# Gradients of shift and scale of the second LayerNorm from column sums in the MLP phase, and gW1 from modulated rows

## The chip, the core and the metric

The kernel runs on one core of a Trainium2 chip. The metric is the device time of one execution in microseconds; several executions are timed and the median is given. A profile of one more execution shows what each engine did. The engines are PE (matrix multiplies; weight loads are listed apart as PEld), DVE (vector), ACT (scalar functions), POOL, and SP, which in this kernel issues every DMA transfer, one after the other in one queue.

## The reference

One block with two branches, forward and backward. `x` is 2048 x 512, the hidden size of the MLP is 1792; everything is bfloat16, the sums fp32.

```python
sa, ca, ga, sb, cb, gb = split(silu(c) @ w_mod)            # six rows of 512
x1  = x  + ga * A(layernorm(x)  * (1 + ca) + sa)           # A: irfft2(rfft2(h) * W)
n2  = layernorm(x1)
h2  = n2 * (1 + cb) + sb                                   # modulated rows
hid = relu(h2 @ w1 + b1) ** 2
out = x1 + gb * (hid @ w2 + b2)
# outputs: out, and the gradients of x, w_r, w_i, w1, b1, w2, b2, c, w_mod for a given grad_out
```

With `gh` for the gradient at the input of the ReLU (2048 x 1792) and `G = gh @ w1.T` for that of `h2`, the gradients of `w1`, of the shift `sb` and of the scale `cb` are

```python
gW1 = h2.T @ gh
gsb = column sums of G            # = sum over f of w1[d, f] * gb1[f],  gb1 = column sums of gh
gcb = column sums of G * n2       # = sum over f of w1[d, f] * (n2.T @ gh)[d, f]
```

The equalities in the comments are the two ways in which the kernels get them.

## The kernel before

The rows are cut into 16 tiles t of 128 rows, and these into 4 blocks b of 4 tiles (SB = 512 rows). The hidden size is 14 tiles fc of 128. A tile scheduler takes the program as it is written in Python, gives each instruction its priority from there and puts each engine's instructions in an order by its own model; the engines then run these lists in order, and SP's list is the order of the transfers. `merge` interleaves lists of pieces, `Delayed(n)` holds n pieces back until later ones come.

In time the kernel has these parts: the forward spectral branch and the product of grad_out with w2 (to about 95 us), the MLP phase (95 to 321), the backward spectral branch with the gradient of w1 between its steps (321 to 424, here the gW1 phase), and the rest: the last inverse transform, the gradient of w2 and that of w_mod (424 to 514).

*MLP phase.* First w1T (the transposed w1, 14 x 128 x 512) is prepared on DVE: times (1 + cb), less its mean over the row (L685 to L691), so that a product with it comes out as the gradient of the normalized row less its mean. Then, per block:

- `stage_h` (L762): 56 matmuls of 128x128 by 512 (L770) into the two PSUM accumulators `mm`, ReLU on ACT (L771), square and product on DVE (L773, L777), both written to DRAM (L778, L779). Its operand h2T is the block's modulated rows, transposed.
- `stage_o` (L829): row tiles of the MLP's output (L788, L790), evicted by ACT (`o`, L842), multiplied by grad_out to `gp` and added to x1, which goes out at L853. Between its pieces runs `stage_g` (L707) of the next block: the last two steps of the forward transform (psT, psY, helper lines L332 to L346), y on ACT (L717), then x1, mean, variance and the normalized rows n2rows on DVE (L734), written to DRAM at L736.
- `stage_gn` (L792): 56 matmuls with w1T (L790, form `og<-w1T,gab`), scaled on ACT to cb (L806), then DVE: a dot product with n2rows (L809), gx1 (L811, L815), the product qy (L820). Between them `stage_t` (L740) of the next block transposes n2rows on PE, 16 tiles into `pst` (L746); DVE (L749) and ACT (L751) evict them with scale and shift: that is h2T.
- `colsums` (L679): three rows (gp, qy, grad_out) summed over the tile into three quadrants of one PSUM tile `acc`.

In the last blocks the first step of the backward transform (`spec_f1_row`) is interleaved as well; for the first two blocks `f1_again` (L858) loads gx1 back from DRAM (L865).

*gW1 phase.* 16 units `grad_w1(fb, dc)` (L941), each 16 matmuls of 128x128 by 448 (L948) with the rows n2 (`n2_sb`, 2 MB, loaded at L986) as operand. DVE makes from the accumulator gW1 (L954, with `gtmp` from ACT L952) and its product with a slice of w1 (`w1s`, loaded per unit), summed to gcb (L956); a third product (L960) gives gsb. `grad_b1` (L921) sums gh over the rows ahead of each four units. The spectral steps of a group gi are psB (L274), AE on ACT (L281, L283), psC (L261) with the factors LFb (L977), G on ACT (L263), and complex products on DVE with the loaded Z and Xb. Two units follow each group from the second on (`fill_w1`), and two are left for the end phase.

*End phase.* A loop over t with the last transform; `fill` puts one piece of `grad_w2` (L1022) into each step, and every second time one row's share of w_mod's gradient (`gm.emit`, L406 to L425). `grad_mod_mid` (L1032) turns the sums gsb and gcb, which lie in columns, into rows first.

Of the kernel before, what the change touches and what calls it, by code (L numbers as in the profile page):

```python
# [428 lines left out]
def kernel(  # L429
# [9 lines left out]
    n2_dram = dram.tile([P, NT, D], BF16, name="n2_dram")  # L439
# [28 lines left out]
    modb = constp.tile([P, 4, D], BF16, name="modb")  # L468
    GA_B, GB_B, CA1_B, CB1_B = range(4)
# [70 lines left out]
    srow = p0.tile([1, 2, D], BF16, name="srow")  # L540

    def mod_row(j):
# [3 lines left out]
        if j in (1, 4):  # L546
            nc.vector.tensor_scalar(modb[:, CA1_B if j == 1 else CB1_B, :], ps, 1.0, None, op0=ALU.add)
        elif j in (2, 5):
            nc.scalar.copy(out=modb[:, GA_B if j == 2 else GB_B, :], in_=ps)
        else:  # L550
            nc.scalar.copy(out=srow[:, j // 3, :], in_=ps[0:1, :])
# [36 lines left out]
    for i in range(4):  # L588
        nc.tensor.matmul(psc[:, i, :], lhsT=srow[:, 0, i * P:(i + 1) * P],
                         rhs=pm, start=True, stop=True)  # L590
# [9 lines left out]
    for i, row in enumerate((srow[:, 1, :], modb[0:1, CB1_B, :], modb[0:1, GB_B, :])):  # L600
# [66 lines left out]
    b2row = wp.tile([1, D], BF16, name="b2row")  # L667
    nc.sync.dma_start(b2row, B_b2[None, :])
    rows = tc.alloc_tile_pool(name="rows", bufs=2)
    hring = tc.alloc_tile_pool(name="hring", bufs=8)  # L670
# [3 lines left out]
    with tc.tile_pool(name="psR", bufs=1, space=PSUM) as psR, tc.tile_pool(name="psO", bufs=2, space=PSUM) as psO_pool, \  # L674
# [4 lines left out]
        def colsums(t, *trio):  # L679
            for i, row in enumerate(trio):  # L680
# [3 lines left out]

        nmean = wp.tile([P, NFC], FP32, name="nmean")  # L685
        for fc in range(NFC):
            nc.vector.scalar_tensor_tensor(out=w1T[:, fc, :], in0=w1T[:, fc, :], scalar=K["onef"], in1=modb[:, CB1_B, :], op0=ALU.mult, op1=ALU.mult,
                                           accum_out=nmean[:, fc:fc + 1])
        nc.vector.tensor_scalar(nmean, nmean, -1.0 / D, None, op0=ALU.mult)
        for fc in range(NFC):  # L690
            nc.vector.tensor_scalar(w1T[:, fc, :], w1T[:, fc, :], nmean[:, fc:fc + 1], None, op0=ALU.add)  # L691

        h2T, n2b, x1b, yb, hT, gbt, qys, gps = ({} for _ in range(8))
        ghn = [None] * NB
        late = Delayed(2)
# [11 lines left out]
        def stage_g(b):  # L707
# [13 lines left out]
            def norm(j):  # L721
# [10 lines left out]
                rstd_act(nc, inv2[:, t:t + 2], mv[:, :, 1], K)  # L732
                for i in range(2):
                    nc.vector.tensor_scalar(n2b[b][:, j + i, :], x1[:, i, :], mv[:, i, 0:1], inv2[:, t + i:t + i + 1], op0=ALU.subtract, op1=ALU.mult)  # L734
# [3 lines left out]
            return [lambda f=f, j=j: f(j) for j in range(TB) for f in (g2, g3)]  # L738
# [23 lines left out]
        def stage_h(b):  # L762
            sl = slice(b * SB, (b + 1) * SB)
            load_rows(b + 1)
            for fc in range(0, NFC, 2):
# [13 lines left out]
                nc.sync.dma_start(gh_dram[fc * P:(fc + 2) * P, sl].rearrange("(a p) s -> p a s", p=P), gh)  # L779

        def sums(t):
            if t in gps and t in qys:
                for t in (t, t + 1):
                    late.add(lambda t=t: colsums(t, gps[t], qys[t], gbt[t // TB][:, t % TB, :]))
# [7 lines left out]
        def stage_gn(b, ub=None):  # L792
            P_, st = {}, {}

            def half(j, h):
                t = TB * b + j
                if j % 2 == 0 and h == 0:
                    st["gx1"] = rows.tile([P, 2, D], BF16, name="gx1")
                    st["cb"] = rows.tile([P, 2, D], BF16, name="cb", bufs=3)
# [3 lines left out]
                if h == 0:  # L803
                    return
                i, gx1, cb, n2row, gb = j % 2, st["gx1"], st["cb"], n2b[b][:, j, :], gbt[b]
                nc.scalar.activation(cb[:, i, :], P_.pop(j), AF.Copy, scale=inv2[:, t:t + 1])  # L806
                jk = rows.tile([P, D], BF16, name="jk", bufs=1)
                rb = rows.tile([P, 1], FP32, name="rb")
# [358 lines left out]
```

## Time and profile before

| | before |
|---|---|
| median of 3 runs | 516.03 us (514.89 to 520.2) |
| profiled execution, its own time | 516.24 us |
| its span, first to last instruction | 514.5 us |
| mean granted clock of PE | 0.954 |
| busy: PE / DVE / ACT | 453.1 / 363.1 / 239.5 us |
| bytes moved by DMA | 99.39 MB |

The profile gives names of tiles as the program has them, without buffer numbers; where a name ends in a digit the digit is left out too (n2_sb shows as n_sb, w1s as w1s). A wait of an engine is put down to the instruction that ended it. The granted clock is the share of full speed at which PE was let run in a window.

### The profile page before, as it was taken

The numbers are of one execution on the slowest core, as the hardware profiler recorded it, in microseconds if no ns is written. First come the engines' busy times: TensorE is split into PE (matmuls) and PEld (weight loads), VectorE is DVE, ScalarE is ACT, GpSimd is POOL, SyncE is SP. The second block draws the span as 40 slices with busy tenths as digits, with TensorE's granted clock in tenths as the row PEclk, the third lists the DMA queues.
The fourth block names the chain that finished last, engine by engine and source line by source line (L and its number), as shares of the span: only waits on it lengthen the run. The fifth ranks groups of instructions, "written<-read, shape, count | busy, mean of one in ns | idle before, by whom it ended". The sixth has DMA issues, their size and how long they took to land.

```text
span 514.5 us, 7304 instructions
## 1 busy us (share of the span) xinstructions
PE 453.1 (88%) x2507; PEld 226.1 (44%) x2507; DVE 363.1 (71%) x862; ACT 239.5 (47%) x415; POOL 12.5 (2%) x56
## 2 busy tenths in 40 slices
PE   0868999999999999989999799766986999879995
PEld 0434466554434444444444344543442465434342
DVE  5877899685479863867487462357796578469986
ACT  3455766683551361455237232653222257627424
POOL 4111100000000000000000000000000000000000
PEclk9957999999999999999999889889998899989998
DMA  8954859921394495399039746676556519988997
GB/s 286 235 159 97 328 139 295 336 73 42 119 302 151 134 295 145 125 199 331 22 111 249 233 109 137 193 237 150 142 139 219 169 45 280 236 256 263 250 261 234
DMA packets 148062, 99.39 MB, mean 193 GB/s; under 512 B 93363, under 2 KB 134841, under 8 KB 147385
## 3 DMA queue, kind: packets, MB, share of 16 engines
q1 hardware_dynamic: 148024, 98.93, 68.8%
q8 instruction: 19, 0.31, 0.2%
q14 instruction: 19, 0.15, 0.1%
HBM read 37.26 MB, written 39.61 MB: 149 GB/s over the span
## 4 chain that ended last, share of the span: by engine, by line
PE 56%; DVE 17%; DMA 11%; SPq 8%; ACT 5%; issue 3%; DVEq 0%; ACTq 0%
PE og L790 16%; PE mm L770 9%; PE mm L621 7%; PE mm L948 6%; PE psG L301 3%; SPq L516 3%; DMA w1s<-in_B_w_dram 2%; PE psY L346 2%; PE psT L332 2%; PE psB L274 2%; SPq L518 2%; PE psC L261 2%; DVE jk L1092 2%; DMA n<-n_dram 1%; DVE gm_junk L423 1%
## 5 line engine op out<-in xcount | busy, mean ns | idle before, releaser
L948 PE MATMUL mm<-gab,n_sb 128*128 128x448 bf16 x256 | 54.4, 372 | 5.7 <-DVE gjk L956 5.7
L621 PE MATMUL mm<-gT,w2T 128*128 128x512 bf16 x224 | 55.4, 380 | 1.9 <-DVE gab L624 1.6
L790 PE MATMUL og<-w1T,gab 128*128 128x512 bf16 x224 | 54.2, 391 | 0.0
L770 PE MATMUL mm<-h2T,w 128*128 128x512 bf16 x224 | 52.8, 378 | 0.1
L1025 PE MATMUL mm<-g_sb,hn 128*128 128x512 bf16 x224 | 51.9, 381 | 0.0
L790 PE MATMUL og<-w,h 128*128 128x512 bf16 x224 | 51.4, 380 | 0.0
L771 ACT ACTIVATE r<-mm,b1col 128x512 bf16<-128x512 f32 x56 | 38.2, 688 | 13.1 <-PE mm L770 9.4
L948 PEld LDWEIGHTS <-n_sb 128*128 128x128 bf16 x256 | 26.0, 102 | 33.9 <-issue 14.0
L770 PEld LDWEIGHTS <-w 128*128 128x128 bf16 x224 | 21.3, 97 | 28.4 <-issue 6.7
L790 PEld LDWEIGHTS <-gab 128*128 128x128 bf16 x224 | 22.1, 101 | 24.8 <-issue 3.6
L621 PEld LDWEIGHTS <-w2T 128*128 128x128 bf16 x224 | 21.5, 98 | 25.3 <-issue 5.9
L1025 PEld LDWEIGHTS <-hn 128*128 128x128 bf16 x224 | 21.1, 98 | 26.1 <-issue 3.8
L790 PEld LDWEIGHTS <-h 128*128 128x128 bf16 x224 | 20.8, 98 | 26.0 <-issue 2.9
L624 DVE CAST gab<-mm 128x512 bf16<-128x512 f32 x28 | 19.2, 687 | 15.6 <-PE mm L621 15.4
L773 DVE TENSOR_TENSOR h<-r 128x1024 bf16<-128x1024 bf16 x28 | 19.3, 690 | 15.0 <-ACT r L771 14.9
L842 ACT CAST o<-og 128x512 bf16<-128x512 f32 x16 | 9.4, 586 | 42.6 <-PE og L790 42.6
L847 DVE TENSOR_TENSOR gp<-gb,o 128x1024 bf16<-128x1024 bf16 x8 | 5.5, 689 | 28.7 <-ACT o L842 28.7
L335 ACT ACTIVATE Tsb<-psT 128x512 bf16<-128x512 f32 x32 | 18.3, 600 | 14.2 <-PE psT L332 14.1
L954 DVE SCALAR_TENSOR_TENSOR gw<-mm,mcol,gtmp 128x448 bf16<-128x448 f32 x16 | 10.9, 681 | 19.5 <-PE mm L948 18.5
L626 ACT CAST gab<-mm 128x512 bf16<-128x512 f32 x28 | 16.4, 586 | 16.2 <-PE mm L621 16.2
L806 ACT ACTIVATE cb<-og,inv 128x512 bf16<-128x512 f32 x16 | 11.0, 688 | 26.8 <-PE og L790 26.8
L952 ACT ACTIVATE gtmp<-gb1bc,mcol 128x448 f32<-128x448 bf16 x16 | 10.3, 665 | 22.8 <-DVE gw L954 22.7
(270 smaller groups left out, 813.7 us busy)
## 6 DMA issues: line engine op xcount, KB each, us to landing
h_dram<-h SPq DMA_DIRECT2D x28, 256.0 KB, 3.1
gh_dram<-gab SPq DMA_DIRECT2D x28, 256.0 KB, 3.3
w<-in_B_w_dram SPq DMA_DIRECT2D x2, 1792.0 KB, 8.0
wm<-in_w_mod_dram SPq DMA_DIRECT2D x3, 1024.0 KB, 8.9
wmc<-in_w_mod_dram SPq DMA_DIRECT2D x12, 256.0 KB, 4.4
out_dram<-gwm SPq DMA_DIRECT2D x12, 256.0 KB, 3.9
xs_dram<-Xs SPq DMA_DIRECT2D x8, 258.0 KB, 3.0
Xb<-xs_dram SPq DMA_DIRECT2D x8, 258.0 KB, 3.0
```

Source lines behind the costliest of these rows:

```text
L301: nc.tensor.matmul(ps[:, ch, :], lhsT=Z[gi][:, hh, ri, ch:256:2], rhs=K["LG"][:, n, ri:ri + 2, :].rearrange("p y m -> p (y m)"), start=(ri ...
L335: nc.scalar.activation(Tsb, ps, AF.Copy, scale=EF_S)
L516: nc.sync.dma_start(gT[b][:, :, j * P:(j + 1) * P], g_view[:, TB * b + j, :], transpose=True)
L621: nc.tensor.matmul(ps, lhsT=w2T[:, dc, fc * P:(fc + 1) * P], rhs=gT[b][:, dc, :], start=(dc == 0), stop=(dc == 3))
L624: nc.vector.tensor_copy(out=gaT[b][:, fc, :], in_=ps)
L626: nc.scalar.copy(out=gaT[b][:, fc, :], in_=ps)
L770: nc.tensor.matmul(ps, lhsT=w1[:, dc, (fc + i) * P:(fc + i + 1) * P], rhs=h2T[b][:, dc, :], start=(dc == 0), stop=(dc == 3))
L771: nc.scalar.activation(r[:, i, :], ps, AF.Relu, bias=b1col[:, fc + i:fc + i + 1])
L773: nc.vector.tensor_tensor(h2, r, r, op=ALU.mult)
L790: nc.tensor.matmul(ps, lhsT=lhs(fc), rhs=rhs[:, fc, :], start=(fc == 0 and init is None), stop=(fc == NFC - 1))
L948: nc.tensor.matmul(ps[:, 0:W4], lhsT=n2_sb[:, t, dc * P:(dc + 1) * P], rhs=ghn[t // 4][:, t % 4, fs], start=(t == 0), stop=(t == NT - 1))
L1025: nc.tensor.matmul(ps, lhsT=hns[fc][:, t, :], rhs=g_sb[:, t, :], start=(t == 0), stop=(t == NT - 1))
```

## The change

1. *MLP phase.* w1T stays as loaded. `stage_gn` evicts the plain product G (the gradient of the modulated row) on ACT; a new function `norm_back` works on two tiles at a time and makes q2 = G * n2 and v = G * (1 + cb), takes the mean of v (ACT, with an accumulator) and the dot product with n2 (DVE), and puts gx1 together from n2, scaled and shifted by ACT, from v and from grad_out. `colsums` takes four rows (gp, qy, G, q2), so that sums 3 and 4 are gsb and gcb.
2. `stage_g` makes n2 on ACT, and on DVE two products more, the modulated rows h2r, which are written to DRAM (h2_dram) in pairs. For blocks 1 to 3 h2T is read from there by a transposing DMA, one for each tile; block 0 stays with `stage_t`. The transposing loads of gh (`ghn_part`) move from `stage_o` to `stage_gn`. The first products of `late` are held in two lists, both emptied after the third pair of `stage_h`; `f1_again` loads two pairs ahead. The buffers of h go from 8 to 7, those of gp from 3 to 2.
3. *gW1 phase.* The units use the modulated rows (`h2_sb`), so their accumulator is gW1 itself: one ACT copy, and one write for two units. The slices w1s and the three DVE passes go. Each four units' `grad_b1` comes after them, not ahead.
4. *End phase.* The sums of shift and scale are rows already. Grad_out's column sums (for b2's gradient), no longer summed in the MLP phase, become 16 matmuls of their own (`grad_b2`). Five rows of w_mod's gradient are in the list (gms) instead of four entries, so one more stands behind the loop.

The core of the diff:

```diff
-        def colsums(t, *trio):
-            for i, row in enumerate(trio):
+        def colsums(t, *quad):
+            for i, row in enumerate(quad):
...
-        for fc in range(NFC):
-            nc.vector.scalar_tensor_tensor(out=w1T[:, fc, :], in0=w1T[:, fc, :], scalar=K["onef"], in1=modb[:, CB1_B, :], op0=ALU.mult, op1=ALU.mult,
-                                           accum_out=nmean[:, fc:fc + 1])
...
                 for i in range(2):
-                    nc.vector.tensor_scalar(n2b[b][:, j + i, :], x1[:, i, :], mv[:, i, 0:1], inv2[:, t + i:t + i + 1], op0=ALU.subtract, op1=ALU.mult)
-                if j == TB - 2:
-                    nc.sync.dma_start(n2_dram[:, TB * b:TB * b + TB, :], n2b[b])
+                    nc.scalar.activation(n2b[b][:, j + i, :], x1[:, i, :], AF.Identity, bias=nb[:, i:i + 1], scale=inv2[:, t + i:t + i + 1])
...
+                nc.vector.tensor_tensor(h2r, n2b[b][:, j:j + 2, :], modb[:, CB1_B, None, :].broadcast_to([P, 2, D]), op=ALU.mult)
+                nc.vector.tensor_tensor(h2r, h2r, modb[:, SB_B, None, :].broadcast_to([P, 2, D]), op=ALU.add)
+                nc.sync.dma_start(h2_dram[:, t:t + 2, :], h2r)
+                if b > 0:
+                    for i in range(j, j + 2):
+                        nc.sync.dma_start(h2T[b][:, :, i * P:(i + 1) * P], h2_dram[:, TB * b + i, :], transpose=True)
...
+                if h == 1:
+                    nc.scalar.copy(out=st["G"][:, j % 2, :], in_=P_.pop(j))
+                    if j % 2 == 1:
+                        norm_back(t - 1, j - 1)
+
+            def norm_back(t, j):
...
+                nc.vector.tensor_tensor(q2, G, n2, op=ALU.mult)
+                nc.vector.tensor_tensor(v, G, cb1[:, None, :].broadcast_to([P, 2, D]), op=ALU.mult)
+                for i in range(2):
+                    nc.scalar.activation(v[:, i, :], v[:, i, :], AF.Copy, scale=i2[:, i:i + 1], accum_out=rr[:, 0, i:i + 1])
+                    nc.vector.scalar_tensor_tensor(out=jk[:, i, :], in0=q2[:, i, :], scalar=K["onef"], in1=cb1, op0=ALU.mult, op1=ALU.mult,
+                                                   accum_out=rr[:, 1, i:i + 1])
...
+                for i in range(2):
+                    nc.scalar.activation(n2[:, i, :], n2[:, i, :], AF.Identity, scale=rr[:, 1, i:i + 1], bias=rr[:, 0, i:i + 1])
+                nc.vector.tensor_tensor(v, v, gb, op=ALU.add)
+                gx1 = n2
+                nc.vector.tensor_tensor(gx1, gx1, v, op=ALU.add)
...
-            nc.vector.scalar_tensor_tensor(out=gw, in0=ps[:, 0:W4], scalar=mcol[:, CB1_C, dc:dc + 1], in1=tmp, op0=ALU.mult, op1=ALU.add)
...
-            nc.vector.scalar_tensor_tensor(out=jk, in0=ps[:, 0:W4], scalar=K["onef"], in1=w1s, op0=ALU.mult,
-                                           op1=ALU.mult, accum_out=gcba[:, dc, fb:fb + 1])
...
+        nc.scalar.copy(out=w1o[0][:, fb % 2, :], in_=ps[:, 0:W4])
+        if fb % 2 == 1:
+            nc.sync.dma_start(out4_view[:, dc, (fb - 1) * W4:(fb + 1) * W4], w1o[0].rearrange("p a f -> p (a f)"))
...
-        nc.sync.dma_start(n2_sb, n2_dram)
+        nc.sync.dma_start(h2_sb, h2_dram)
...
+    def grad_b2():
+        ps = psX.tile([P, D], FP32, name="mm")
+        for t in range(NT):
+            q = 32 * (t % 4)
+            nc.tensor.matmul(ps[q:q + 32, :], lhsT=K["ones_q"], rhs=g_sb[:, t, :], start=(t < 4), stop=(t >= 12), tile_position=(0, q))
+        add_quadrants(ps, gwp, out_7[None, :], modb[0:1, GB_B, :])
```

The scheduler's lists move with it. At the change from block 2 to block 3, ACT's list (L806 is the eviction of the w1 product, L807 in the new kernel; L771 and L772 are the ReLU of stage_h; utcs belongs to the first spectral step). Before:

```order
L806 ACTIVATE cb<-og,inv_70 128x512
L751 ACTIVATE h2T<-pst_2860,mcol 128x512
L806 ACTIVATE cb<-og,inv_70 128x512
L239 CAST utcs<-psY 128x64x8
L751 ACTIVATE h2T<-pst_2893,mcol 128x512
L806 ACTIVATE cb<-og,inv_70 128x512
L771 ACTIVATE r<-mm,b1col 128x512 x4
L239 CAST utcs<-psT 128x64x8
L239 CAST utcs<-psY 128x64x8
L771 ACTIVATE r<-mm,b1col 128x512 x10
```

and after (v and n2rows are written by norm_back):

```order
L807 CAST G<-og 128x512 x2
L822 ACTIVATE v,rr<-v,inv_70 128x512 x2
L807 CAST G<-og 128x512
L828 ACTIVATE n2rows<-n2rows,rr 128x512 x2
L807 CAST G<-og 128x512
L239 CAST utcs<-psY 128x64x8
L822 ACTIVATE v,rr<-v,inv_70 128x512 x2
L772 ACTIVATE r<-mm,b1col 128x512 x2
L828 ACTIVATE n2rows<-n2rows,rr 128x512 x2
L772 ACTIVATE r<-mm,b1col 128x512 x4
```

Four passes of norm_back stand among the first ReLUs. On PE, in the new kernel, the first column sum (gp) stands ahead of the 56 matmuls of stage_h, and those of y, G and q2 of the first pair behind the second of them, at each of the block changes (at the third with a piece of the spectral step on v ahead of them).

SP's list ahead of the same change, where the rows of block 3 are written (L736; in the new kernel h_dram<-h2r stands for h2_dram, L734, and the transposes into h2T are L737; out_dram<-x is stage_o's output, gx_dram the gradient of the rows, gab<-gh_dram the transposing loads of gh). Before:

```order
L853 DMA out_dram<-x_2043 128x1024 x2
L736 DMA n_dram<-n2rows 128x2048
L816 DMA gx_dram<-gx_2778 128x1024
L865 DMA gx_3082<-gx_dram 128x1024
L760 DMA_TRANSPOSE gab<-gh_dram 128x4x256 x4
```

and after:

```order
L869 DMA out_dram<-x_2025 128x1024
L880 DMA o<-gx_dram 128x1024
L734 DMA h_dram<-h2r 128x1024
L737 DMA_TRANSPOSE h2T<-h_dram 128x4x128 x2
L869 DMA out_dram<-x_2025 128x1024
L880 DMA o<-gx_dram 128x1024
L734 DMA h_dram<-h2r 128x1024
L737 DMA_TRANSPOSE h2T<-h_dram 128x4x128 x2
L832 DMA gx_dram<-n2rows 128x1024
L761 DMA_TRANSPOSE gab<-gh_dram 128x4x256 x6
```

What h2T needs goes through this queue now, each half behind a write of stage_o's output.

SP's list at the start of the gW1 phase (n_sb is n2_sb, h_sb is h2_sb; LFb, Z and Xb are operands of the spectral steps). Before:

```order
L977 DMA LFb<-LF_dram 128x768 x2
L493 DMA Z_3387<-in_A_w_r_dram 64x2x257
L493 DMA Z_3387<-in_A_w_r_dram 32x2x257 x2
L493 DMA Z_3387<-in_A_w_i_dram 64x2x257
L493 DMA Z_3387<-in_A_w_i_dram 32x2x257 x2
L980 DMA Xb<-xs_dram 128x1032
L493 DMA Z_3388<-in_A_w_r_dram 64x2x257 x2
L493 DMA Z_3388<-in_A_w_i_dram 64x2x257 x2
L980 DMA Xb<-xs_dram 128x1032
L986 DMA n_sb<-n_dram 128x8192
```

and after:

```order
L869 DMA out_dram<-x_2460 128x1024
L989 DMA LFb<-LF_dram 128x768 x2
L998 DMA h_sb<-h_dram 128x8192
L869 DMA out_dram<-x_2460 128x1024
L989 DMA LFb<-LF_dram 128x768 x3
L493 DMA Z_3384<-in_A_w_r_dram 64x2x257
L493 DMA Z_3384<-in_A_w_r_dram 32x2x257 x2
L493 DMA Z_3384<-in_A_w_i_dram 64x2x257
L493 DMA Z_3384<-in_A_w_i_dram 32x2x257 x2
L992 DMA Xb<-xs_dram 128x1032
```

The 2 MB of rows for gW1 now come ahead of Z and Xb and of all but two pieces of LFb.

More of the change, by code (lines that the diff above doesn't have):

```diff
@@ L963 @@
     units = []
-    for fb in range(NFB):
+    for fp in range(0, NFB, 2):
         for dc in range(4):
-            units.append(lambda fb=fb, dc=dc: (dc == 0 and grad_b1(fb), grad_w1(fb, dc)))
+            for fb in (fp, fp + 1):
+                units.append(lambda fb=fb, dc=dc: (grad_w1(fb, dc), dc == 3 and grad_b1(fb)))
     def fill_w1(n):
@@ L1030, in grad_w2 @@
         load_hn()
-    def grad_mod_mid(i, j):
-        psr = psX.tile([P, D], FP32, name="mm")
-        for dc in range(4):
-            nc.tensor.matmul(psr[0:1, dc * P:(dc + 1) * P], lhsT=colsb[:, i, dc:dc + 1], rhs=K["ident"], start=True, stop=True)
-        row = gwp.tile([1, D], BF16, name="gmrow")
-        nc.scalar.copy(out=row, in_=psr[0:1, :])
-        gm.emit(j, 0, row, endp["gm"], psX)
+    def grad_b2():
[4 more added lines that the diff above has]
+        add_quadrants(ps, gwp, out_7[None, :], modb[0:1, GB_B, :])
     load_hn()
```

163 lines of the change are left out of this document (77 added, 86 removed).

## The prediction

> **What bounds the kernel now.** I read the page first, then the windows of three long stretches, then the waits of PE in the one where PE is least busy, and last the timeline around its longest gaps.
>
> ```profile
> span 514.5 us, 7304 instructions
> PE 453.1 (88%) x2507; PEld 226.1 (44%) x2507; DVE 363.1 (71%) x862; ACT 239.5 (47%) x415; POOL 12.5 (2%) x56
> 321.00:424.00 103.00, 83.38 (x542) 46.51 (x540) 69.81 (x157) 38.63 (x67) 0.00 (x0) 0.92 0.56 161
> ```
>
> In the last line stand the window, its length, then busy time of PE, its weight loads, DVE, ACT and POOL, the granted clock of PE, the DMA share and GB/s. PE is the bound as a whole, so what counts is where PE stands idle or runs at a lower clock. The gW1 phase (321 to 424) is the weak place: 83.38 of 103 us busy, at a granted clock of 0.92. The waits of PE in it, and four rows of its timeline (start, duration, in brackets the idle time before):
>
> ```profile
> PE psB L274 <- ACT AE L283: 6.1, 5, 2.2
> PE mm L948 <- DVE gjk L956: 5.7, 2, 4.0
> PE psC L261 <- ACT G L263: 2.3, 1, 2.3
> PE mm L934 <- DVE gjk L956: 1.8, 2, 1.3
> PE psC L261 <- DMA LFb<-LF_dram: 1.6, 1, 1.6
> PE mm L935 <- DVE b4l L932: 1.4, 2, 1.3
> PE mm L927 <- DVE gjk L956: 0.7, 1, 0.7
> 346.25 6.22 PE L948 MATMUL mm<-gab,n_sb 128*128 128x448 bf16 x32
> 357.95 7.90 PE L948 MATMUL mm<-gab,n_sb 128*128 128x448 bf16 x32 [1.66 <-DVE gjk L956]
> 397.28 7.96 PE L948 MATMUL mm<-gab,n_sb 128*128 128x448 bf16 x28 [4.04 <-DVE gjk L956]
> 396.53 0.69 DVE L956 SCALAR_TENSOR_TENSOR gjk<-mm,onef,w1s 128x448 bf16<-128x448 f32 x1 [3.52 <-DMA w1s<-in_B_w_dram]
> ```
>
> The seven waits are 19.6 us. Those on DVE are 5.7 + 1.8 + 1.4 + 0.7 = 9.6: a PSUM accumulator of gW1 comes free only after the product L956, and that product waits for the slice w1s (the last row: 3.52 us, behind which the 4.04 us gap of PE stands). Those on the spectral chain (ACT, and the LFb load) are 10.0. Behind a gap the same work is also slower: 32 matmuls take 6.22 us, but 7.90 after the gap of 1.66 (1.68 lost), and 28 take 7.96 after 4.04, where 28/32 of 6.22 is 5.44 (2.5 lost). So 4.2 us of clock loss belong to the DVE gaps, 13.8 us together.
>
> **gW1 phase.**
>
> ```profile
> 366.45 0.75 PE L927 MATMUL mm<-gab,ones_q 128*32 128x448 bf16 x12
> n_sb<-n_dram SPq DMA_DIRECT2D x1, 2048.0 KB, 8.8
> L842 ACT CAST o<-og 128x512 bf16<-128x512 f32 x16 | 9.4, 586 | 42.6 <-PE og L790 42.6
> ```
>
> The three DVE passes over each unit (L954, L956, L960), gtmp on ACT and the w1s loads go; an ACT copy of PSUM comes. The 13.8 us go with their cause. The copy of 448 columns is at most the 0.59 us that one of 512 takes (L842): 14 units in the phase give ACT some 8 us, in place of 14 gtmp, and ACT stays far below PE. What is late next is the copy itself: on ACT it stands behind G (L263) and AE, and the accumulators are two. Bounds: nothing, and 14 units times 0.59, some 8; I take 3, nearest to the one wait on G above (2.3).
>
> Two of the four grad_b1 now follow g1. One is 16 quadrant matmuls (12 in 0.75, so about 1.0), two full ones (0.2 each by 346.25) and the half of the 1.4 us wait on b4l that falls to two of them, 1.7 us as an estimate. So 3.4 us leave this phase and come back later. The 2 MB load of modulated rows took 8.8 us in the form n_sb, and was issued behind both Z and Xb; now it stands right behind two LFb pieces, so the first unit can start earlier than 346.25 and fill some of the 10.0 us of spectral waits. But it pushes three LFb pieces and Z back by up to its own 8.8. Bounds: all 10 filled, or 5 lost; I take 3.5 gained. Sum of the phase: -13.8 - 3.4 - 3.5 + 3 = -17.7, ends about -8 and -24.
>
> The skill page "TensorE: Matmul & The Clock Gate" (the Trainium skill, Part 1, the HAM clock gate) says that the clock halves after an idle window of about 3.4 us; by it the gap of 1.66 would have cost no clock, and the sum would be 1.7 us smaller. The trace does not agree: 7.90 against 6.22 us after 1.66 us idle.
>
> **MLP phase, what goes.**
>
> ```profile
> L687 DVE SCALAR_TENSOR_TENSOR w1T<-w1T,onef,modb 128x512 bf16<-128x512 bf16 x14 | 9.5, 747 | 1.0 <-DMA gh_dram<-gab 1.0
> 150.00:177.00 27.00, 27.00 (x132) 11.64 (x132) 24.21 (x65) 6.22 (x10) 0.00 (x0) 1.00 0.51 172
> PE psT L232 <- DVE gx L866: 2.9, 1, 2.9
> PE pst L746 <- DVE h2T L749: 0.7, 1, 0.7
> PE pst L746 <- DVE n2rows L734: 0.7, 2, 0.4
> PE psT L332 <- ACT Tsb L335: 1.5, 2, 0.7
> 223.70 0.39 PE L746 MATMUL pst<-ident,n2rows 128*128 128x128 bf16 x4
> 223.93 0.59 PE L770 MATMUL mm<-h2T,w 128*128 128x512 bf16 x2
> 293.90:297.30 3.40, 3.35 (x12) 1.80 (x13) 3.26 (x7) 1.17 (x2) 0.00 (x0) 0.50 0.05 13
> 297.30:300.70 3.40, 3.40 (x11) 1.35 (x10) 0.98 (x2) 0.56 (x1) 0.00 (x0) 0.61 0.40 141
> ```
>
> The preparation of w1T (L687, 9.5 us and the smaller passes) lies at 150 to 177, where PE is busy 27.00 of 27.00: worth nothing by itself, whatever DVE saves. Four transposes occupy PE for 0.23 us (223.70 to 223.93); 48 go, 12 x 0.23 = 2.8. The waits around them go, 0.7 + 0.7, and of the 1.5 on Tsb, which stand at the same place, between the transposes, I take 1.1: 2.5. The f1 stage of the last two blocks waits 2.9 for its load (L866); the loads are now issued two pairs ahead, so that goes, and the clock behind it: 3.40 us at 0.50 and 3.40 at 0.61 lose 1.7 + 1.3 = 3.0. Together 2.8 + 2.5 + 2.9 + 3.0 = 11.2.
>
> **MLP phase, what comes.** The durations:
>
> ```profile
> L771 ACT ACTIVATE r<-mm,b1col 128x512 bf16<-128x512 f32 x56 | 38.2, 688 | 13.1 <-PE mm L770 9.4 <-ACT r L771 0.6 <-DVE n2rows L734 0.4
> L1085 ACT ACTIVATE gs<-gn,inv 128x512 bf16<-128x512 bf16 x16 | 11.4, 716 | 1.1 <-DVE gn L1083 1.1
> L1085 ACT ACTIVATION_READ_ACCUMULATOR gs<-gn,inv 128x1 f32 x16 | 3.1, 193 | 0.0
> L572 ACT ACTIVATE x_sb<-x_sb,l_nb,inv 128x512 bf16<-128x512 bf16 x8 | 6.1, 804 | 6.4 <-DVE l_nb L566 6.4
> L815 DVE TENSOR_TENSOR gx<-gx,cb 128x1024 bf16<-128x1024 bf16 x8 | 5.5, 690 | 0.2
> 275.58 7.43 PE L770 MATMUL mm<-h2T,w 128*128 128x512 bf16 x32
> 282.85 1.24 PE L790 MATMUL og<-w1T,gab 128*128 128x512 bf16 x5
> ```
>
> A matmul of the MLP takes (282.85 - 275.58)/32 = 0.227 us, so four, one relu's worth, 0.91. Take the last pair of stage_gn, whose last matmul ends at 0; stage_h of the next block follows it at once. ACT copies G to 0.59 (as L842); DVE makes q2 and v (2 x 0.69) to 1.97; ACT scales v with its accumulators (2 x 0.91) to 3.79, and the second relu stands behind that on ACT, so it ends at 4.48. Meanwhile PE has filled both accumulators at about 2.7 and waits to 4.48: 1.8 us. Then the two Identity passes on n2 (2 x 0.80) go to 6.09, ahead of the third relu, to 6.78; PE, done with the one free accumulator at 5.4, waits 1.4 more. The column sums that stand there give it about 0.5 us of work, and y of the first pair may be late for these. I take 2.8 for each of three handovers, 8.4 (bounds: 0, where the sums and the first matmuls cover all, and 9 each, the rival below).
>
> The handover of h2T:
>
> ```profile
> 213.68 0.59 ACT L717 CAST y<-psY 128x512 bf16<-128x512 f32 x1 [0.71 <-PE psY L346]
> 220.95 0.73 DVE L734 TENSOR_SCALAR n2rows<-x,l_mv,inv 128x512 bf16<-128x512 bf16 x2
> h_dram<-h SPq DMA_DIRECT2D x28, 256.0 KB, 3.1
> gT<-in_grad_out_dram SPq DMA_TRANSPOSE x16, 2.8
> SPq L853 <- DVE x L852: 14.6, 3, 7.9
> ```
>
> From the last y to n2 of the last pair are 221.68 - 213.68 = 8.0 us; ACT's Identity in place of DVE's passes adds 0.9, the two products to h2r 1.4: 10.3. The write takes 3.1, and the second of two transposes lands between 2.8 and 5.6 after it (both at once, or one behind the other), 4.2 taken: 17.6. In that time PE has the rest of stage_o (about 21 matmuls) and all 56 of stage_gn, 77 x 0.227 = 17.5. It fits by a hair; I take 1.5 each at blocks 2 and 3, 3.0 (bounds 0 and 6 each). SP's gab transposes stand behind h2T, its out_dram<-x ahead of it (a rival below). ACT's passes on n2 (0.80 in place of 0.37) lie under stage_o and stage_gn in three blocks, where a stage like 150 to 177 has ACT busy 6.22 of 27; in the first block nothing of the MLP covers them, and the last four are 4 x 0.43 = 1.7 late, of which two lie beside other rows' work: 1.0. The fourth column sum has a quadrant of its own, at most 16 x 0.06 by the row at 366.45, taken as 0. The ring of h, 7 buffers for 8, holds one block's seven pairs, and 56 matmuls of stage_gn lie between their last reading and the next writing: 0. norm_back costs DVE about what the old chain did, with more handing over, which is in the 2.8. Sum of what comes 8.4 + 3.0 + 1.0 = 12.4; net of the phase +1.2 (ends -10 and +12).
>
> **End phase.**
>
> ```profile
> 453.58 0.59 PE L1089 MATMUL acc<-q,ones_q 128*32 128x512 bf16 x1 [4.86 <-DVE q L1086]
> ```
>
> Two grad_b1 arrive (3.4), grad_b2 comes (16 quadrant matmuls and two one-row ones, 1.7), the eight matmuls and two copies of grad_mod_mid go (-1.0, an estimate: two copies of at most 0.59 each). The gap of 4.86 stands where DVE waits for a load of n1; with PE work behind g1 some of it is covered, 1.6. One gm.emit is later, behind other work. Sum +2.5 (ends -3 and +6).
>
> **The sum:** +1.2 - 17.7 + 2.5 = -14.0; 514.5 - 14.0 = 500.5 of span. The profiled run took 516.24, 1.74 more than its span, and lies 0.2 above the median of 516.03: 500.5 + 1.7 = **502 us**.
>
> **The rivals.**
> *The gW1 evictions are late on ACT.* PE waited 2.3 us for G on ACT already, and now every accumulator of gW1 stands behind it. If half of the 13.8 comes back and nothing of the spectral waits is filled: 502 + 6.9 + 3.5 = 512. For it: ACT is in order, and there are two accumulators. Against: ACT is busy only 38.63 of 103.
> *The handover serializes (slower).* The sums over y, G and q2 stand two matmuls into stage_h in PE's order. y of a pair is ready 0.59 + 1.38 + 1.82 + 1.61 and four products (2.76) after its last matmul, 8.2 us, with DVE's share of other work more like 9. If each handover waits that in full, 3 x 9 + 3 x 3.0 of clock (as after 293.90) is 36 in place of 8.4: 502 + 27.6 = 530. It decides from about 7.5 us lost at each handover, clock included: 3 x (7.5 - 2.8) = 14, the whole gain. For it: the chain goes four times between ACT and DVE. Against: the first pair has 28 matmuls (6.4 us) of cover.
> *h2T is late (slower).* If the transposes' SP entries wait behind out_dram<-x (14.6 us of such waits on SP, longest 7.9, in the last row of the h2T fence) or h2r comes only at the end of stage_gn, 3.1 + 2.8 are bare at three blocks, and 3.0 of clock each: 502 - 3.0 + 17.7 + 9.0 = 526. The Trainium skill speaks for this one: "VectorE: DVE Perf Modes", Rules for kernel authors, says to transpose 128x128 by TensorE where PSUM will do, else by the DMA crossbar, and its table gives 390 and 1309 ns; no run here has this transpose in both forms. Against: 17.5 us of matmuls lie over it.
> *DVE was not what PE waited for in gW1:* then the gaps go to the spectral chain, and only the MLP's terms are left, 516.
>
> **The chances.** Forecast 0.67, late evictions 0.15, serial handover 0.08, late h2T 0.05, no effect 0.05. The forecast's own range, with its ends not all at once, is 490 to 512. The range 488 to 513 leaves out the two slow cases, the last one and the tails, near 0.2. A measurement here can tell about 1% from no change, 510.9 to 521.2. Faster: 0.67 less a tail, and nearly half of the late evictions, 0.73; same 0.14; slower 0.13.
>
> **What would show it.** Waits of PE on an L956 kind of DVE product gone from the gW1 phase, PE busy over 90% there, first unit before 346: the first step. If in its place PE's gW1 matmuls wait for ACT's copy, the first rival. Waits of the stage_h matmuls on relu of 2 to 3 us at each of three block changes: my second step; on a DMA transpose of h2T: the third rival; PE column sums on y for over 5 us: the second. The wait at f1's load and the clock of 0.50 behind it must be gone. The prediction is wrong if the gW1 phase is not at least 8 us shorter, or if the MLP phase is more than 12 longer.

## The result and the profile after

The changed kernel takes 502.14 us in the median (499.89 to 503.18, four runs) beside 517.19 for the kernel before (514.89 to 520.2): a ratio of 0.970, with a 95% interval of 0.963 to 0.977. The profiled execution has a span of 501.3 us, 13.2 less than before. The page's first rows, then the windows of three stages (window, length, busy PE, PEld, DVE, ACT, POOL, granted clock, DMA share, GB/s): the MLP phase from the first matmul of stage_h to the last of stage_o, the gW1 phase from the first spectral step to the last, and the end phase.

```profile
span 501.3 us, 7176 instructions
PE 444.4 (89%) x2485; PEld 220.8 (44%) x2485; DVE 327.9 (65%) x747; ACT 264.8 (53%) x474; POOL 12.4 (2%) x56
134.55:311.29 176.74, 171.94 (x847) 76.69 (x849) 113.08 (x217) 98.54 (x173) 0.14 (x2) 1.00 0.79 203
311.80:399.10 87.30, 75.89 (x496) 43.10 (x492) 40.67 (x82) 32.89 (x60) 0.00 (x0) 0.92 0.60 167
399.10:501.30 102.20, 86.58 (x485) 39.63 (x477) 68.07 (x161) 52.13 (x105) 0.00 (x0) 0.96 0.86 226
```

The same stages of the kernel before:

```profile
135.63:320.59 184.96, 178.24 (x880) 79.84 (x881) 122.38 (x254) 77.17 (x123) 0.14 (x2) 0.98 0.67 185
321.06:421.67 100.61, 80.99 (x530) 45.27 (x527) 68.33 (x155) 37.40 (x65) 0.00 (x0) 0.92 0.57 163
421.67:514.50 92.83, 82.02 (x438) 38.69 (x431) 68.98 (x170) 48.43 (x99) 0.00 (x0) 0.97 0.93 249
```

| stage | before | after | difference | predicted |
|---|---|---|---|---|
| ahead of the MLP phase | 135.6 | 134.6 | -1.0 | +1.0 |
| MLP phase | 185.0 | 176.7 | -8.2 | +0.2 |
| gW1 phase | 100.6 | 87.3 | -13.3 | -17.7 |
| end phase | 92.8 | 102.2 | +9.4 | +2.5 |
| span | 514.5 | 501.3 | -13.2 | -14.0 |

The prediction's +1.2 for the MLP phase counted from 95 us, so the 1.0 us that it took for late passes of ACT in the first block stands in the first row here. The total was hit, but not by its terms: the MLP phase gained 8.4 us more than its sum, the gW1 phase 4.4 less, and the end phase lost 6.9 more, outside its bounds of -3 and +6. How much of this belongs to a single execution is told with the experiments. What PE waits for in the new gW1 phase (total, times, longest):

```profile
PE psC L261 <- DMA LFb<-LF_dram: 4.3, 1, 4.3
PE psB L274 <- ACT AE L283: 3.5, 3, 1.5
PE psG L301 <- DVE utcs L306: 2.4, 1, 2.4
PE mm L966 <- DMA h_sb<-h_dram: 1.2, 1, 1.2
```

Its timeline at three of these places (start, duration, idle time before in brackets):

```profile
322.20 2.79 PE L966 MATMUL mm<-gab,h_sb 128*128 128x448 bf16 x7 [1.20 <-DMA h_sb<-h_dram]
356.99 0.61 PE L261 MATMUL psC<-AE,LFb 128*128 128x257 bf16 x2 [4.30 <-DMA LFb<-LF_dram]
357.99 5.65 PE L966 MATMUL mm<-gab,h_sb 128*128 128x448 bf16 x16
```

No wait on a DVE product of gW1 is left, and none on its new ACT copy. PE is busy 75.89 of 87.30 us, 87%, short of the 90% that the prediction named as a sign. For the piece of LFb PE now waits 4.3 us, where it waited 1.6 for one before, with 2.5 us of half clock behind it (16 matmuls in 5.65, where 32 take 6.2), and 2.4 us for DVE are new. The piece of LFb is the sixth of eight. SP issues it just ahead of its use, while the kernel before had issued all eight within 5 us of the start of the phase. The row of SP for this piece, and the last one of the kernel before:

```profile
352.34 1.06 SPq L989 DMA_DIRECT2D LFb<-LF_dram  x1
325.02 0.83 SPq L977 DMA_DIRECT2D LFb<-LF_dram  x2
```

In the MLP phase these waits are left:

```profile
PE mm L771 <- DMA h2T<-h_dram: 1.9, 2, 1.2
PE psT L232 <- DVE v L834: 1.5, 1, 1.5
PE mm L771 <- ACT r L772: 0.5, 1, 0.5
```

And the end phase has its gap on the load of n1 still, 6.43 us beside 4.86 before, and a new one near the end. PE's timeline at both:

```profile
433.93 0.59 PE L1097 MATMUL acc<-q,ones_q 128*32 128x512 bf16 x1 [6.43 <-DVE q L1094]
491.51 3.61 PE L1037 MATMUL mm<-g_sb,hn 128*128 128x512 bf16 x16 [1.84 <-DVE gw L1040]
```

and SP's issues ahead of the first:

```profile
402.20 13.57 SPq L1032 DMA_TRANSPOSE hn<-h_dram  x3
420.88 8.50 SPq L1032 DMA_TRANSPOSE hn<-h_dram  x3
429.43 0.59 SPq L1080 DMA_DIRECT2D n<-n_dram  x1
```

The load of n1 is issued at 429.43 us, right behind the transposing loads of hn, which hold SP until then.

### The profile page after: what moved, and what is told of

Same layout as the page of the kernel before. It is cut to its first block, busy times and chain, and to the rows that moved or that the text cites. A ratio compares the mean times of both kernels' runs of the same rounds, so it can differ in the third digit from the quotient of the medians.

```text
span 501.3 us, 7176 instructions
## 1 busy us (share of the span) xinstructions
PE 444.4 (89%) x2485; PEld 220.8 (44%) x2485; DVE 327.9 (65%) x747; ACT 264.8 (53%) x474; POOL 12.4 (2%) x56
## 5 line engine op out<-in xcount | busy, mean ns | idle before, releaser
L966 PE MATMUL mm<-gab,h_sb 128*128 128x448 bf16 x256 | 54.3, 370 | 1.2 <-DMA h_sb<-h_dram 1.2
L771 PE MATMUL mm<-h2T,w 128*128 128x512 bf16 x224 | 52.9, 379 | 2.6 <-DMA h2T<-h_dram 1.9
L794 PE MATMUL og<-w1T,gab 128*128 128x512 bf16 x224 | 50.3, 379 | 0.0
L772 ACT ACTIVATE r<-mm,b1col 128x512 bf16<-128x512 f32 x56 | 37.9, 685 | 15.1 <-PE mm L771 10.2
L966 PEld LDWEIGHTS <-h_sb 128*128 128x128 bf16 x256 | 25.6, 102 | 26.0 <-issue 4.8
L771 PEld LDWEIGHTS <-w 128*128 128x128 bf16 x224 | 21.1, 97 | 32.2 <-issue 9.2
L970 ACT CAST gw<-mm 128x448 bf16<-128x448 f32 x16 | 8.5, 533 | 31.5 <-PE mm L966 31.5
L423 DVE SCALAR_TENSOR_TENSOR gm_junk<-wmc,onef,gmbc 128x512 bf16<-128x512 bf16 x24 | 17.9, 748 | 8.2 <-DMA wmc<-in_w_mod_dram 7.1
L379 DVE TENSOR_TENSOR p<-Z,G 128x1028 bf16<-128x1028 bf16 x8 | 5.6, 699 | 25.9 <-ACT AE L283 13.5
L545 PE MATMUL mod_ps<-wm,scb 128*128 128x512 bf16 x24 | 9.6, 515 | 10.9 <-DVE scb L536 7.7
```

What stands on the lines that cost most here:

```text
L423: nc.vector.scalar_tensor_tensor(out=junk, in0=wmc[:, i, :], scalar=K["onef"], in1=gmbc, op0=ALU.mult, op1=ALU.mult, accum_out=self.gsc[:, ...
L771: nc.tensor.matmul(ps, lhsT=w1[:, dc, (fc + i) * P:(fc + i + 1) * P], rhs=h2T[b][:, dc, :], start=(dc == 0), stop=(dc == 3))
L772: nc.scalar.activation(r[:, i, :], ps, AF.Relu, bias=b1col[:, fc + i:fc + i + 1])
L794: nc.tensor.matmul(ps, lhsT=lhs(fc), rhs=rhs[:, fc, :], start=(fc == 0 and init is None), stop=(fc == NFC - 1))
L966: nc.tensor.matmul(ps[:, 0:W4], lhsT=h2_sb[:, t, dc * P:(dc + 1) * P], rhs=ghn[t // 4][:, t % 4, fs], start=(t == 0), stop=(t == NT - 1))
```

## The experiments

Ratios are to the kernel before, with 95% intervals; the changed kernel stands at 0.970. The stages quoted are those of one profiled execution each. A stage that an edit leaves alone shows the noise of such an execution. The changed kernel's gW1 phase, left alone by an edit, was 82.9 to 87.3 us in four kernels; of these 4.4 us, 1.9 are PE's busy time at a lower clock and 2.4 the wait for DVE, which the shortest does not have. Its MLP phase was 176.7 to 177.4, its end phase 100.0 to 102.2. In the kernel before and the two built on it, the end phase was 92.8 to 95.3, and the MLP phase of the first experiment, at full clock, 182.4 in place of 185.0:

```profile
136.11:318.49 182.38, 174.40 (x862) 78.79 (x881) 122.31 (x254) 77.08 (x123) 0.14 (x2) 1.00 0.71 188
```

So of the differences in the table, the MLP phase's is 5 to 6 us without the clock, the gW1 phase's 13 to 18, and the end phase's 5 to 9.

**The products over gW1, taken from the kernel before.**

```diff
-        w1s = gwa.tile([P, W4], BF16, name="w1s", bufs=3)
-        nc.sync.dma_start(w1s, w1_view[:, dc, fs])
...
-            nc.vector.scalar_tensor_tensor(out=jk, in0=ps[:, 0:W4], scalar=K["onef"], in1=w1s, op0=ALU.mult,
-                                           op1=ALU.mult, accum_out=gcba[:, dc, fb:fb + 1])
...
-        nc.vector.scalar_tensor_tensor(out=jk, in0=w1s, scalar=K["onef"], in1=gb1bc, op0=ALU.mult, op1=ALU.mult,
-                                       accum_out=gsba[:, dc, fb:fb + 1])
```

> The kernel before without the two products over each gW1 unit (L956, L960) and without the slices w1s that they read; the gradients of shift and scale of the second LayerNorm, and with them two rows of w_mod's gradient and part of c's, are left out (zeros). Theory (the gW1 term of the prediction): PE's 9.6 us of waits on DVE and the 4.2 us of clock behind them go, 13.8 us, ratio to before 0.973 (0.967 to 0.98). Rival (the spectral chain takes their place): under 5 us, ratio 0.99 or more, with longer waits on AE, G or LFb in the gW1 phase.

Measured: 505.64 us, ratio 0.983 (0.976 to 0.990), between the two. The gW1 phase (319.0 to 409.0) is 10.6 us shorter. PE's waits in it:

```profile
PE psC L261 <- DMA LFb<-LF_dram: 7.6, 2, 4.9
PE mm L948 <- DMA n_sb<-n_dram: 2.2, 1, 2.2
PE psB L274 <- ACT AE L283: 1.5, 2, 1.1
PE mm L937 <- DVE b4l L934: 0.8, 1, 0.8
```

and the issue on SP that moved:

```profile
319.38 0.42 SPq L980 DMA_DIRECT2D n_sb<-n_dram  x1
```

The 9.6 us of waits on DVE are down to 0.8, those on AE and G from 8.4 to 1.5; in their place stand 7.6 on LFb (1.6 before) and 2.2 on the rows. Both theories hold a part: the products, with the slices that they read, were the cause of the waits on DVE, and loads took half of the place. The edit does not name these loads, but the scheduler moved them: the 2 MB load went ahead of Z, Xb and six of the eight pieces of LFb (issued at 319.38, 0.4 us into the phase; 335.28, 14.2 us into it, before), and four pieces of LFb went out only from 356.36 on, where all eight had gone out by 325.9. The two waits on LFb end at 359.62 and 375.86, behind pieces issued at 356.36 and 371.63: it is the late pieces that PE waits for, issued 37 us and more after the 2 MB load.

**The loads of f1_again two pairs ahead, in the kernel before.** The edit is the function `load` of the change, put into the kernel before, with its first two calls ahead of the last `stage_h`.

> The kernel before with only the loads of f1_again issued two pairs ahead. Theory: the wait of 2.9 us on gx L866 goes and with it 3.0 us at the lower clock, 5.9 us, ratio 0.989. Rival (what is next late on PE or a colder clock elsewhere takes it): 1 us or less, ratio 0.998.

Measured: 513.78 us, ratio 0.996 (0.992 to 1.000): about 2 us, below the 5.9 expected. The wait did not go, it fell from 2.9 to

```profile
PE psT L232 <- DVE o L865: 1.6, 1, 1.6
```

which is the product behind the load: DVE itself waits for that load until 293.22 us, and PE until 293.97. The MLP phase is 181.3 us, 1.1 below the 182.4 above, which also has the full clock. And the 3.0 us of clock were not the gap's to give: see the last section.

**h2T on PE again, in the changed kernel.**

```diff
-                if b > 0:
-                    for i in range(j, j + 2):
-                        nc.sync.dma_start(h2T[b][:, :, i * P:(i + 1) * P], h2_dram[:, TB * b + i, :], transpose=True)
...
-                merge(stage_gn(b, UT), parts + [lambda: None])
+                ps_ = parts + [lambda: None] * (7 - len(parts))
+                ts_ = [lambda: None] * 2 + stage_t(b + 1) + [lambda: None]
+                merge(stage_gn(b, UT), [x for p in zip(ts_, ps_) for x in p])
```

> The changed kernel with h2T of blocks 1 to 3 made by PE again (16 transposes a block, evicted by DVE and ACT with scale and shift) instead of transposing DMAs; h2r is still made and written. Theory: 2.8 us of transposes and some waits for their evictions come back, the 1.9 us of waits on the transposing DMA go: 1 to 5 us more than the changed kernel, ratio to before 0.973 to 0.981. Rival (the skill's rule, transposes belong on PE): no slower than the changed kernel, ratio 0.97 or less.

Measured: 498.92 us, ratio 0.972 (0.963 to 0.982): not slower, as the rival said. The MLP phase:

```profile
134.24:309.06 174.82, 172.54 (x874) 79.31 (x893) 115.73 (x223) 102.91 (x179) 0.14 (x2) 1.00 0.73 196
```

It is 1.9 us shorter than with the DMA, as much as the waits on h2T, which are gone. PE is busy 0.6 us longer by the records kept; some of its matmuls are missing in this trace. A later kernel with PE transposes repeats the stage (174.89, below), with PE busy 1.7 longer. The Trainium skill ("VectorE: DVE Perf Modes", Rules for kernel authors) says to transpose 128x128 on TensorE where a destination in PSUM will do. This stage agrees, by some 2 us; the times as a whole do not tell the two apart.

**More work for ACT in norm_back.**

```diff
+                for i in range(2):
+                    nc.scalar.activation(jk[:, i, :], v[:, i, :], AF.Identity, scale=rr[:, 1, i:i + 1], bias=rr[:, 0, i:i + 1])
```

> The changed kernel with two more ACT passes of 128x512 in each norm_back (1.5 us of ACT, eight times, 12 us in all), whose result nobody reads. The prediction's term of 8.4 us said that ACT's passes hold up the first ReLUs of stage_h: then three block changes cost 1.5 us each or more, 4.5 us, ratio to before 0.979. Rival (other work of PE covers them, as the small waits of the changed profile suggest): under 1.5 us, ratio 0.97 to 0.973.

Measured: 500.76 us, ratio 0.973 (0.967 to 0.980). The time is the rival's. In its profile the MLP phase is 178.72 us, 1.3 to 2.0 longer than the others. The group of the new passes (busy time, mean ns):

```profile
L830 ACT ACTIVATE yg<-v,rr 128x512 bf16<-128x512 bf16 x16 | 12.0, 800 | 0.0
```

and PE's wait on the ReLU:

```profile
PE mm L771 <- ACT r L772: 1.9, 4, 1.2
```

It was 0.5. So the squeeze on the ReLU exists, but with 12.0 us more of ACT it is 1.9 us, where 8.4 was predicted without them.

**All of LFb first; gc_t early; LFb behind the 2 MB load; n1 ahead.** The four edits, in this order:

```diff
+        for gi in range(8):
+            nc.sync.dma_start(K["LF"][:, 2 * gi:2 * gi + 2], LF_dram[:, 2 * gi:2 * gi + 2])
...
         def load(gi):
-            nc.sync.dma_start(K["LF"][:, 2 * gi:2 * gi + 2], LF_dram[:, 2 * gi:2 * gi + 2])
...
-        t1 = fp.tile([P, 4], FP32, name="gc_t1")
+        t1 = constp.tile([P, 4], FP32, name="gc_t1")
...
         def load(gi):
-            nc.sync.dma_start(K["LF"][:, 2 * gi:2 * gi + 2], LF_dram[:, 2 * gi:2 * gi + 2])
+            if gi < 2:
+                nc.sync.dma_start(K["LF"][:, 2 * gi:2 * gi + 2], LF_dram[:, 2 * gi:2 * gi + 2])
...
         nc.sync.dma_start(h2_sb, h2_dram)
+        for gi in range(2, 8):
+            nc.sync.dma_start(K["LF"][:, 2 * gi:2 * gi + 2], LF_dram[:, 2 * gi:2 * gi + 2])
...
+        load_n1(0)
+        load_n1(2)
         for t in range(0, NT, 2):
+            load_n1(t + 4)
+            n1, gxl = nl.pop(t)
```

> The changed kernel with all eight pieces of LFb issued at the start of the gW1 phase; on SP the 2 MB load of the modulated rows then stands behind Z and Xb, as in the kernel before. The prediction's term said that the early load is worth 3.5 us (bounds 10 gained, 5 lost). If it is worth that or more, this kernel is no faster than the changed one, 502 us or more, with the first unit of gW1 later than 330 us and longer waits on AE and G. If the late pieces of LFb cost more than the early load gives (the 4.3 us wait, and 2.5 us of clock behind it), it is 2 to 6 us faster, 496 to 500.

> The changed kernel with the four small steps to the derivative of silu (gc_t) in a tile that shares its memory with nothing, so that DVE makes them at the start of the kernel. In the changed profile DVE waits 3.4 us ahead of gc_t for a write of gW1 to leave its buffer, and PE 2.4 us for utcs behind it, with some 1.9 us of clock after. Theory: these go, 2.4 to 4.3 us, 498 to 500. Rival (the end phase starts earlier but waits for its loads): under 1 us.

> The changed kernel with the later six pieces of LFb issued right behind the 2 MB load, which keeps its early place. Theory: the 4.3 us wait on LFb and the 2.5 us of clock behind it go, 6.8 us, ratio to before 0.957. Rival (Z and Xb, now behind them, are late instead, and G with them): 2 us or less, 0.967.

> The changed kernel with the loads of n1 and gxl of the end phase issued two pairs ahead, in three buffers. The prediction took 1.6 us off the gap behind the n1 load; the changed profile has 6.4 in place of 4.9. Theory: the wait is the place of the load behind the transposes of hn on SP; ahead of them it goes, 6.4 us and some 2 of clock, ratio 0.954. Rival (SP is full there, so the transposes come late instead and grad_w2 waits for hn): 2 us or less, 0.967.

Measured: 496.02 (0.959, 0.951 to 0.968), 499.0 (0.965, 0.957 to 0.974), 499.41 (0.967, 0.960 to 0.975) and 494.91 us (0.959, 0.952 to 0.967). All four intervals reach to that of the changed kernel (0.963 to 0.977), so what each is worth by itself is read from the stages and is not firm.

LFb first puts the 2 MB load back behind Z and Xb, and the first unit at 22.4 us into the phase (10.4 in the changed kernel), and yet the phase is 1.3 to 5.7 us below the range given above. Its window:

```profile
311.90:393.50 81.60, 71.89 (x497) 41.95 (x493) 40.64 (x82) 33.01 (x60) 0.00 (x0) 0.98 0.64 179
```

and what is left of PE's waits on the loads and ACT:

```profile
PE psB L274 <- ACT AE L283: 7.6, 7, 1.5
```

The waits on AE are 7.6 us, where the changed kernel with its early rows has 3.5, so the early rows do fill waits of this kind, as the prediction had it. But they come in pieces of at most 1.5, and there is no wait on LFb. With LFb behind the 2 MB load, the wait on LFb goes as well though the rows stay early: it hung on the late place of the LFb pieces, not on the 2 MB ahead of them. Another wait takes its place:

```profile
PE mm L953 <- DVE b4l L950: 4.9, 1, 4.9
```

This product, b4l, stands on DVE behind products that wait for Z until 352.58 us. In the changed kernel it was done at 355.8, 1.2 us ahead of PE's first matmul with the late piece of LFb: the two waits lay on one another, and taking one away gives little. This kernel's phase is 84.3 us, in the range of the changed one, and 2.7 longer than with LFb first and the rows late; in these profiles the early place of the rows gains nothing. gc_t early leaves no wait on utcs in the phase, but its two runs do not separate it from the changed kernel. n1 ahead (load_n1 issues the two loads into three buffers each) has an end phase of 96.8 us, 3.2 to 5.4 below the range above. Its window, and then what is left of the gap in PE's waits:

```profile
394.20:491.00 96.80, 85.53 (x482) 39.09 (x477) 67.99 (x165) 51.50 (x105) 0.00 (x0) 0.99 0.95 250
```

```profile
PE acc L1107 <- DVE q L1104: 3.4, 2, 2.4
```

**grad_b1 ahead of its units again, in the changed kernel.**

```diff
-                units.append(lambda fb=fb, dc=dc: (grad_w1(fb, dc), dc == 3 and grad_b1(fb)))
+                units.append(lambda fb=fb, dc=dc: (dc == 0 and grad_b1(fb), grad_w1(fb, dc)))
```

> The changed kernel with grad_b1 ahead of its units again, as before the change. The prediction moved 3.4 us from the gW1 phase to the end phase and counted no net effect. Theory now (the phase before the first unit has idle time of PE that these sums fill, the end phase has none to spare): end phase 3.4 shorter, gW1 phase 0 to 2 longer, 499 to 501, ratio to before 0.966. Rival (the prediction: one for one): 501 to 503, ratio 0.97.

Measured: 501.61 us, ratio 0.973 (0.969 to 0.977): the rival, which is the prediction's own term. Beside the ranges above, the end phase is 2.7 to 4.9 us shorter and the gW1 phase 1.4 to 5.8 longer, so one for one is possible and not shown. The window of the end phase, and PE's waits on LFb, which have doubled:

```profile
403.50:500.80 97.30, 83.39 (x445) 38.82 (x441) 66.29 (x159) 49.52 (x101) 0.00 (x0) 0.95 0.91 238
```

```profile
PE psC L261 <- DMA LFb<-LF_dram: 8.8, 3, 3.5
```

**The edits together.** First the three on loads and gc_t; then also h2T on PE; then also grad_b1 first and `if gms:` in place of `if gms and n % 2 == 1:`.

> The changed kernel with the three edits that each took a wait away: all LFb loads first (and with them the rows for gW1 behind Z and Xb), gc_t in a tile of its own, n1 and gxl two pairs ahead. If the three add up (6, 3 and 7 us), 486, ratio 0.94; if they lie on one another (DMA is busy throughout these phases), 490 to 494, ratio 0.95.

> The kernel with those three edits, and h2T of all blocks made by PE. Theory after the first run of this (PE waited 2 us less for h2T, the transposes cost no more than that): 0 to 3 us below the kernel with the three edits. The prediction's term said 1 to 5 us above it.

> As the one before, with grad_b1 ahead of its units and with one row of w_mod's gradient at every step of the end loop, not every second, so that fewer stand behind it. In the changed profile DVE waits 7.1 us for the last loads of w_mod and PE 1.8 for DVE, just ahead of the end. Theory: 3 us from grad_b1 and 2 to 3 from the tail, 5 below. Rival (DVE and SP are full in the loop, so the loop gets longer by as much): 3 below or less.

Measured: 492.06 us (0.9545, 0.951 to 0.958), 492.14 (0.9542, 0.950 to 0.958) and 507.34 (0.985, 0.982 to 0.989). The first is 10 us below the changed kernel, less than the 16 of its parts: they lie in part on one another, as its second case said. The windows of its gW1 and end phases, and that of the second one's MLP phase:

```profile
312.10:392.60 80.50, 71.92 (x497) 42.15 (x494) 40.59 (x78) 33.09 (x60) 0.00 (x0) 0.98 0.61 168
392.60:490.60 98.00, 85.58 (x481) 39.08 (x477) 67.37 (x161) 51.57 (x105) 0.00 (x0) 0.98 0.95 247
```

```profile
137.55:312.44 174.89, 173.67 (x891) 79.28 (x893) 115.72 (x223) 102.92 (x179) 0.14 (x2) 1.00 0.75 196
```

The third lost 15 us against the second. In the profiles the gW1 phase is 12.4 longer (94.0 against 81.6) and the end phase 5.3, while what stands ahead of them is 3.3 shorter, mostly in the stretch ahead of the MLP phase, which was 133.5 to 137.6 us in all kernels. Its waits there:

```profile
PE mm L950 <- DVE b4l L947: 5.0, 3, 3.5
PE psG L301 <- DMA LGb<-LG_dram: 2.4, 1, 2.4
PE mm L1036 <- DVE gw L1039: 5.1, 3, 2.3
```

In the gW1 phase the low part of the bias sums waits on DVE, and LGb is late; near the end grad_w2's evictions share DVE with the products of w_mod's gradient. Which of the two edits does what is not settled: only grad_b1 first was run by itself, without the edits on the loads.

## Why the prediction was right, and where its terms were not

The time came out right by luck in part: one mechanism held, and the errors of the other terms cancelled.

- **The gW1 products.** Right in mechanism, mis-sized in the net. The step "the 13.8 us go with their cause" holds for the waits (9.6 to none), and the first experiment shows the products, with their slices, as the cause. But the gain that they alone give was 10.6 us of the phase, since loads took part of the place; and of the 4.2 us of clock in that step, 1.7 need not hang on the products (the last section has the rows). The phase as a whole is 13.3 us shorter in this profile, and 13 to 18 by the range above, so its sum of 17.7 may be met.
- **"I take 3.5 gained" for the early rows.** This step failed. The waits on AE did shrink from 6.1 to 3.5, and the one on G from 2.3 to none, but LFb went from 1.6 to 4.3 with 2.5 of clock, and 1.2 came for the rows themselves: 4.9 gained, 6.4 lost. The prediction had priced the three pieces of LFb right behind the 2 MB load, at up to its 8.8 us. PE never waited for these. It waited for the sixth piece, issued at 352.34 us, and the order ahead of the prediction shows only five of the eight.
- **"I take 3" for late evictions.** No wait of a unit on its ACT copy is in the profile: 0. That rival fell with it.
- **"8.4" for three handovers.** This step failed most. The waits on the ReLU are 0.5, and 1.5 more are for `v` of norm_back, once; with half as many passes again for ACT in norm_back, those on the ReLU are 1.9. ACT's order was as predicted; the working put four matmuls after four, with half a microsecond of column sums between. PE's list has other work there that needs no ReLU: eight column sums, the bias products of stage_o (they show as `og<-grow`), spectral steps. That these are the cover is read from the order; no run takes them away. After the twelfth matmul of stage_h PE does these while ACT catches up (its timeline in the changed kernel, at the second block change):

```profile
216.58 2.40 PE L771 MATMUL mm<-h2T,w 128*128 128x512 bf16 x10
219.24 0.38 PE L792 MATMUL og<-grow,ones_sq 1*128 1x512 bf16 x1
219.55 0.61 PE L332 MATMUL psT<-Cf,utcs 128*128 128x256 bf16 x4
220.41 1.04 PE L771 MATMUL mm<-h2T,w 128*128 128x512 bf16 x4
```

- **h2T by DMA.** The wait of 1.9 us is near the 3.0 taken. The gain of 2.8 + 2.5 on the other side was too large: with the transposes back on PE the stage is shorter, not longer, and of the 2.5 of waits around them 0.4 come back. So the transposes alone did not cause these waits; what did, the runs do not show.
- **f1's load and its clock.** 2.9 of wait went to 0.3 in the changed kernel. The 3.0 of clock was not bound to that wait: two other kernels with the same stage, or nearly, have the full clock there.
- **The end phase.** The steps "3.4", "1.7" and "-1.0" make 4.1, and PE's busy time rose by 4.6. The step "1.6 covered" failed: the gap did not shrink. PE's waits there are 4.7 to 6.4 us in the kernels with the change that leave it alone, and 5.1 to 6.7 in those without. Near the end DVE was 1.8 late for grad_w2, after it had itself waited 7.1 for a load of w_mod; one row more of w_mod's gradient stands there, which had been counted at nothing.
- **The rivals.** Serial handover and late h2T would have shown 5 us and more a handover; the longest single wait there is 1.5, and the worst of the three has 3.2 in all. "DVE was not what PE waited for" falls with the first experiment.

## What to carry to other kernels

A sum that comes out right says little of its terms: here the MLP phase was some 8 us better than its sum, the end phase 2 to 7 worse and the gW1 phase up to 4 worse, and they cancelled. A stall worked out between two queues has to be read against the whole list of the waiting engine, since any independent work in it can be cover. And where a scheduler orders a shared queue, removing work on one engine can move loads on another, large ones ahead and small ones far behind: follow each load to its own issue first, then look at the work saved.

## What the runs showed of the hardware

A gap of the same length can cost clock or not. The kernel before waits 2.94 us at f1's load and runs the next 3.40 us at 0.50; with the edit on gW1 alone the same place has a gap of 2.88 and the full clock behind it. The window of the former (the clock is its third number from the end) stands in the prediction, at 293.90; of the latter, a row of PE's timeline and two windows, one from within the gap and the next:

```profile
294.37 0.28 PE L232 MATMUL psT<-TA,gx 128*128 128x256 bf16 x1 [2.88 <-DVE gx L866]
```

```profile
293.00:296.40 3.40, 2.03 (x14) 1.35 (x15) 2.67 (x6) 1.07 (x2) 0.00 (x0) 1.00 0.00 0
296.40:299.80 3.40, 3.08 (x18) 1.61 (x18) 3.17 (x7) 0.69 (x1) 0.00 (x0) 1.00 0.43 154
```

In the other direction, a gap of 1.49 us, the last in a row of shorter ones, was followed by spectral steps at half speed (eight in 1.86 us, 1.03 at others), in the kernel with the three edits:

```profile
326.48 1.86 PE L274 MATMUL psB<-Cdb,utcs 128*128 128x256 bf16 x8 [1.49 <-ACT AE L283]
```

The Trainium skill ("TensorE: Matmul & The Clock Gate", Part 1) says that the gate watches a free-running window of some 3.4 us, so that the penalty varies from run to run. That agrees with these rows better than the reading by single gaps in the prediction, where 1.66 us was set against the rule. Just ahead of that gap the kernel before has another:

```profile
355.20 1.09 PE L261 MATMUL psC<-AE,LFb 128*128 128x257 bf16 x8 [2.30 <-ACT G L263]
```

So 3.96 of the 5.05 us before the slow matmuls were idle, and the loss need not be the 1.66 us gap's. In the kernel with only the loads of f1_again moved, where gW1 is as before, the same place has half speed already between the two gaps (1.88 us for the eight, 1.09 above), ahead of the wait on DVE, which is only 0.87 there:

```profile
350.76 1.88 PE L261 MATMUL psC<-AE,LFb 128*128 128x257 bf16 x8 [2.30 <-ACT G L263]
353.51 8.21 PE L954 MATMUL mm<-gab,n_sb 128*128 128x448 bf16 x32 [0.87 <-DVE gjk L962]
```

The 1.7 us that the prediction put down to the products at this place came there without their wait being long. For a sum this means that a clock loss seen once behind a gap of 1.5 to 3 us is not sure to be there, nor to go: some 3 us of the MLP phase's 8.2 is this.
